# Attention and feed-forward on one core: split probabilities transposed by VectorE blocks and SBUF-to-SBUF transfers instead of TensorE

## The chip, the cores and the metric

One NeuronCore of one Trainium2 chip runs the whole program; the other cores are idle. The metric is the device time of one execution in microseconds, as the median of three runs. Engines are named as the profile names them: PE (TensorE matmuls), PEld (TensorE weight loads), DVE (VectorE), ACT (ScalarE), POOL (GpSimd) and SP (SyncE, which issues all DMAs here).

## The reference

Eight batches of eight heads, 576 rows of 64, in float32. Each row of scores keeps only entries within `tau` of its maximum; the attention output, with heads side by side, is 4608 tokens of 512 and goes through a feed-forward layer of width 2048:

```python
scores = scale * np.matmul(q, k.transpose(0, 1, 3, 2))
thresh = np.max(scores, axis=-1, keepdims=True) - tau
scores = np.where(scores >= thresh, scores, -1000000000.0)
scores = scores - np.max(scores, axis=-1, keepdims=True)
attn = np.exp(scores)
attn = attn / (np.sum(attn, axis=-1, keepdims=True) + 1e-09)
attn_out = np.matmul(attn, v)                     # then heads are concatenated: x
r = np.maximum(x @ w_in, 0.0)
out = (s * (r * r) + b) @ w_out
```

## The kernel before

**Number format.** Most operands are split into a high half in the format fp32r and a low half (value minus high half, also fp32r), and a product is the sum of two or three fp32r matmuls. Batch 0 alone is computed with plain float32 matmuls ("plain" tiles), while the weights are still being loaded and split; batches 1 to 7 use "split" tiles.

**Tiles.** A tile is 128 query rows of one head against all 576 keys. There are 288 tiles: 36 plain, 252 split. A batch has two halves of 256 query rows per head, and 64 tail rows per head; two heads' tails share one tile. For each tile, in `tile_of`: PE computes the scores (L329); DVE moves them to `sm`, negated and scaled, with the row minimum (L332), and adds `tau` to it (L335); ACT takes the exponential into `em` (L338); DVE masks it and sums the row (L341), and takes the reciprocal and a small clipping term (L344, L346); POOL normalizes `em` (L349); PE transposes `em` in four blocks of 128x128 and one of 128x64 into the PSUM banks `tp` and `tt` (L358, L359). For a split tile ACT copies the transposed block to the high half (L389, L391) and DVE subtracts it to get the low half (L392, L394). `with_v` multiplies a group of 256 or 320 query columns with v: nine matmuls (L405), of which the last takes the last 64 keys with both halves side by side; ACT and DVE add the two halves of the result (L410, L412).

**Heads.** `Head.load` and `Head.prepare` load k (twice, on both halves of the partitions), q and v of a head, and split them: k on ACT and POOL (L279, L280), q on ACT and DVE (L287, L288), v on ACT and POOL (L292, L293). This is done anew for each half of a batch, so 112 times.

**Feed-forward.** A `Block` takes 256 tokens (18 blocks, 288 steps of 128 hidden units). A step is twelve matmuls of 256 columns (L536) into the bank `h`, three ACT operations (L539, L541, L542), the low half on POOL (L543; on DVE in the last block) and six matmuls of 512 columns (L549). `finish` scales the sum on DVE (L560) and stores it.

**Order.** Each engine runs its instructions in a fixed order. `Plan` makes it before the program is built: every operation has an engine, a planned duration, the keys that it reads and writes, and a due time counted in tiles (`at`); the planner runs through simulated time and gives each engine, when it is free, the ready operation that is due first. DMAs are planned on SP the same way. Operations with `port=True` and all POOL operations are planned never to overlap (L92 to L94); `dve2` sets that mark:

```python
    def dve2(cost, fn, r, w, at):
        plan.add("DVE", cost, fn, r, w, at, True)
```

On the chip nothing but semaphores between dependent operations is left of the plan, and the order. `LOAD_AHEAD`, `PREPARE_AHEAD`, `VALUES_AFTER` and `FFN_AFTER` shift the due times of loads, splits, `with_v` and feed-forward blocks; `each` spaces the steps of a block.

Of the kernel before, what the change touches and what calls it, by code (L numbers as in the profile page):

```python
# [9 lines left out]
F32 = mybir.dt.float32  # L10
# [5 lines left out]

LOAD_AHEAD, PREPARE_AHEAD = 6, 2.5  # L20
SCORES_AHEAD, VALUES_AFTER = 1, 1
FFN_AFTER = 1.5


# [3 lines left out]
FIRST_WEIGHTS = 4  # L28

# [78 lines left out]
def tile_attention_ffn(ctx: ExitStack, tc: tile.TileContext, qT, kT, v, tau, w_in, w_out, s, b, out):  # L108


# [14 lines left out]
    HS = S // 2  # L125

# [19 lines left out]
    st = [const(f"st{i}", [P, 8]) for i in range(6)]
    smem = [tuple(const(f"{n}{i}", [P, S + 1]) for n in ("sm", "em")) for i in range(2)]
    qs = [const(f"q{j}", [P, NB], F32R) for j in range(2)]
    raw_head = const("rk", [P, S]), const("rq", [P, S]), const("rv", [P, 5, D])
    xb = [const(f"x{i}", [P, NC, NB]) for i in range(3)]  # L150
    xt = const("xt", [P, NC, 4 * T])
    oo = const("oo", [P, 2, DM])
# [3 lines left out]
        ("s", [P, 2, 512]), ("o", [P, 2, DM]), ("tp", [P, NQ, P]), ("tt", [P, 512]), ("pv", [P, 512]), ("h", [P, 512]))}  # L156
# [4 lines left out]
    def claim(keys, fn):  # L161

        old = [k for k in list(plan.writer) + list(plan.readers) if isinstance(k, tuple) and k[0] == keys[0]]
        plan.add("-", (0, 0), fn, [], list(dict.fromkeys(old)) + keys, -100)


    def split_buffers():
        def e():
            t = sb("e", [P, 9, 3 * P], F32R)
            lazy["ehi"], lazy["elo"] = t[:, 0:5], t[:, 5:9]  # L170

        def k():
            lazy["k"] = sb("k", [P, 4, S], F32R)

        def v_():
            lazy["v"] = sb("v", [P, 3, 5, 2, D], F32R)
        claim(["e"] + [(n, c) for n in ("eh", "el", "et") for c in range(6)], e)
        claim(["k", "khi0", "klo0", "khi1", "klo1"], k)
        claim(["v", "v0", "v1", "v2"], v_)
        claim(["e32", "oo0", "oo1"] + [("x", 2, c, j, u) for c in range(NC) for j in range(2) for u in range(2)], lambda: None)  # L180

    def pe(n, cols, fn, r, w, at):

        plan.add("PE", (n * (0.44 * cols + 6.5), n * (0.44 * cols + 6.5) + 170), fn, r, w, at)
# [4 lines left out]
    def dve2(cost, fn, r, w, at):  # L189
        plan.add("DVE", cost, fn, r, w, at, True)  # L190
# [9 lines left out]


    class Plain:


        def __init__(self, bi, p_):
            self.bi, self.p, self.tag = bi, p_, ("w%d" % (NF - 1), "v", "k", "e")[p_]
            self.keys = [(self.tag, n) for n in ("k", "q", "v0", "v1")]

        def get(self):
            if self not in lazy:  # L210
                t = sb(self.tag, [P, 2 * S - T + 10 * D], F32)
# [18 lines left out]
        def load_tail(self, at):  # L230
            for j in range(2):
                dma(16, lambda j=j: nc.sync.dma_start(
                    out=qd[self.p % 2][j * D:(j + 1) * D, j * T:(j + 1) * T], in_=qT[self.bi, 2 * self.p + j, :, M:S]),
                    [f"qd{self.p % 2}"], [(f"qd{self.p % 2}", j)], at)

    class Head:
        def __init__(self, i, bi, h, q0, q1, tail):
            self.i, self.bi, self.h, self.j, self.q0, self.q1, self.tail = i, bi, h, h % 2, q0, q1, tail

        def load(self, at):  # L240

            q0, q1 = self.q0, self.q1
            rk, rq, rv = raw_head
            self.parts = [], [], []

            def put(which, name, buf, cols, ap, kb):
                for o in 0, D:
                    keys = [(name, o, c) for c in range(cols.start // T, cols.stop // T)]
                    self.parts[which].extend(keys)
                    dma(kb, lambda o=o: nc.sync.dma_start(out=buf[o:o + D, cols], in_=ap), [], keys, at)  # L250
# [7 lines left out]
            dma(128, lambda: nc.sync.dma_start(out=rv[:, 0:NQ, :],
                                               in_=v[self.bi, self.h, 0:M, :].rearrange("(p t) d -> p t d", t=NQ)),
                [], [("rv", 0)], at)  # L260
            for o in 0, D:
                self.parts[2].append(("rv", 1 + o))
                dma(16, lambda o=o: nc.sync.dma_start(out=rv[o:o + D, NQ, :], in_=v[self.bi, self.h, M:S, :]),
                    [], [("rv", 1 + o)], at)

        def prepare(self, at):
            pk, pq, pv_ = self.parts
            j = self.j
            rk, rq, rv = raw_head
            q0, m = self.q0, self.q1  # L270
            self.kks, self.kqs, self.kts = [f"khi{j}", f"klo{j}"], [f"q{j}"], [f"qt{j}"]

            def khi():
                return lazy["k"][:, 2 * j]

            def klo():
                return lazy["k"][:, 2 * j + 1]
            self.q, self.ks = (lambda: qs[j]), (lambda: [khi(), klo()])
            act((580, 675), lambda: nc.scalar.copy(out=khi(), in_=rk), pk, [f"khi{j}"], at)  # L279
# [156 lines left out]

    def weights(f, at):

# [344 lines left out]
```

## Time and profile before

| | |
|---|---|
| median of three runs | 1404.68 us (1398.01, 1405.58, 1404.68) |
| span of the profiled execution | 1402.1 us (the page gives no other time of that execution) |
| PE, PEld busy | 99%, 89% |
| DVE, ACT, POOL busy | 76%, 70%, 53% |
| DMA engines | 23.5% on the kernel's queue, 71 GB/s |

The page shows one execution. A group row gives an engine's instructions of one line: how often, the busy time, the mean duration, then the idle time just before them and what ended it. Durations of PE matmuls overlap, since matmuls are pipelined: what one costs is the distance from its start to the start of the next. A window row gives the busy time of each engine in one stretch of the span, with the number of instructions.

### The profile page before, as it was taken

Reading aid. Unit: us, or ns where it says so; the run is one execution under the profiler, and the core shown is the slowest. Engines: PE = TensorE matmul, PEld = TensorE weight load, DVE = VectorE, ACT = ScalarE, POOL = GpSimd, SP = SyncE. Lnnn points to the kernel's source line nnn. Section 1 sums busy time; section 2 is a strip of 40 time slices with the busy share of each in tenths; the row PEclk is TensorE's granted clock in tenths of the full one; section 3 lists DMA queues with packets and bytes.
Section 4 is the critical chain, followed back from the end, with each engine's and each line's share of the span. In section 5 each row is a group of like instructions: output and inputs, shape, how many; then the busy total and the mean of one; then the engine's idle time right before and its main releaser. Section 6 shows DMA issues by size and latency. Waiting matters only on the chain.

```text
span 1402.1 us, 29393 instructions
## 1 busy us (share of the span) xinstructions
PE 1384.8 (99%) x9369; PEld 1252.3 (89%) x9369; DVE 1066.8 (76%) x3099; ACT 986.8 (70%) x2487; POOL 736.3 (53%) x798
## 2 busy tenths in 40 slices
PE   9999999999999999999999999999999999999998
PEld 7678789889899989998999999999999999999887
DVE  4977568988998898878888787888788887887101
ACT  3777557867777777777777777777777777776443
POOL 1233336656676656655566555665566555564210
PEclk9999999999999999999999999999999999999999
DMA  9701112221222222222122122222222222220000
GB/s 301 248 26 35 29 39 66 82 74 55 79 74 87 63 76 70 81 60 70 52 84 72 55 73 64 83 60 66 65 71 71 70 66 72 64 75 15 16 16 16
DMA packets 94539, 99.59 MB, mean 71 GB/s; under 512 B 34480, under 2 KB 72368, under 8 KB 94384
## 3 DMA queue, kind: packets, MB, share of 16 engines
q1 hardware_dynamic: 94384, 97.71, 23.5%
q8 instruction: 74, 1.21, 0.4%
q14 instruction: 81, 0.66, 0.1%
HBM read 88.21 MB, written 9.44 MB: 70 GB/s over the span
## 4 chain that ended last, share of the span: by engine, by line
PE 93%; DVE 3%; ACT 2%; issue 1%; POOL 0%; DMA 0%; DVEq 0%; SPq 0%; ACTq 0%; POOLq 0%
PE h L536 28%; PE o L549 28%; PE s L329 12%; PE pv L405 9%; PE tp L358 9%; PE pv L374 3%; PE tt L359 2%; DVE em L341 1%; PE h L677 1%; PE h L488 1%; PE o L329 1%; DVE sm L332 1%; DVE e L392 0%; ACT em L338 0%; ACT g L539 0%
## 5 line engine op out<-in xcount | busy, mean ns | idle before, releaser
L536 PE MATMUL h<-xh,w 128*128 128x256 f32 x2304 | 465.5, 285 | 5.0 <-ACT g L539 4.8
L349 POOL TENSOR_SCALAR em<-em,st 128x576 f32<-128x576 f32 x288 | 251.9, 875 | 273.3 <-DVE st L346 113.2
L536 PEld LDWEIGHTS h<-xh,w 128*128 128x128 f32 x2304 | 376.4, 190 | 15.8 <-ACT g L539 8.9
L549 PE MATMUL o<-w,gh 128*128 128x512 f32 x1152 | 369.6, 402 | 0.6 <-ACT g L539 0.5
L543 POOL TENSOR_TENSOR gl<-g,gh 128x256 fp32r<-128x256 f32 x272 | 217.4, 799 | 263.8 <-ACT gh L542 93.6
L536 PE MATMUL h<-xl,w 128*128 128x256 f32 x1152 | 325.4, 282 | 0.2
L341 DVE SCALAR_TENSOR_TENSOR em<-sm,st,em 128x577 f32<-128x577 f32 x288 | 255.3, 887 | 34.5 <-ACT em L338 25.8
L332 DVE TENSOR_SCALAR_CACHE_REDUCE sm<-s 128x576 f32<-128x576 f32 x280 | 211.2, 754 | 89.2 <-PE s L329 86.9
L338 ACT ACTIVATE em<-sm,st 128x576 f32<-128x576 f32 x288 | 224.9, 781 | 49.2 <-DVE sm L332 44.6
L539 ACT ACTIVATE g<-h 128x256 f32<-128x256 f32 x288 | 109.1, 379 | 187.6 <-PE h L536 184.2
L549 PE MATMUL o<-w,gl 128*128 128x512 f32 x576 | 225.9, 392 | 0.1
L536 PEld LDWEIGHTS h<-xl,w 128*128 128x128 f32 x1152 | 219.1, 190 | 5.7 <-DVE xl L521 0.6
L549 PEld LDWEIGHTS o<-w,gh 128*128 128x128 f32 x1152 | 196.4, 189 | 25.9 <-ACT g L539 0.8
L392 DVE TENSOR_TENSOR e<-tp,e 128x512 fp32r<-128x512 f32 (+1 forms) x280 | 178.0, 636 | 53.7 <-ACT e L389 50.0
L389 ACT CAST e<-tp 128x512 fp32r<-128x512 f32 (+1 forms) x280 | 150.5, 538 | 64.3 <-PE tp L358 59.9
L280 POOL TENSOR_TENSOR k<-rk,k 128x576 fp32r<-128x576 f32 x112 | 169.7, 1515 | 45.3 <-ACT k L279 41.9
L358 PE MATMUL tp<-ident,em 128*128 128x128 f32 x1152 | 175.2, 275 | 1.9 <-POOL em L349 0.8
L329 PE MATMUL s<-k,q 128*128 128x288 f32 x896 | 165.4, 306 | 0.3 <-DVE sm L332 0.3
L358 PEld LDWEIGHTS tp<-ident,em 128*128 128x128 f32 x1152 | 137.1, 140 | 26.3 <-issue 5.4
L405 PE MATMUL pv<-e,v 128*128 128x320 f32 (+1 forms) x1008 | 152.6, 296 | 0.0
L405 PEld LDWEIGHTS pv<-e,v 128*128 128x128 f32 x1008 | 141.4, 189 | 2.3
L329 PEld LDWEIGHTS s<-k,q 128*128 128x128 f32 x896 | 130.1, 189 | 4.4 <-DVE sm L332 0.9
(108 smaller groups left out, 1799.3 us busy)
## 6 DMA issues: line engine op xcount, KB each, us to landing
rk<-in_k_dram SPq DMA_DIRECT2D x224, 144.0 KB, 2.8
rv<-in_v_dram SPq DMA_DIRECT2D x112, 128.0 KB, 2.1
rq<-in_q_dram SPq DMA_DIRECT2D x168, 64.0 KB, 2.3
w<-in_moe_w_in_dram SPq DMA_DIRECT2D x16, 512.0 KB, 8.6
w<-in_moe_w_out_dram SPq DMA_DIRECT2D x16, 512.0 KB, 8.7
out_dram<-oo SPq DMA_DIRECT2D x32, 256.0 KB, 2.2
rq<-in_q_dram SPq DMA_DIRECT2D x56, 80.0 KB, 2.4
rv<-in_v_dram SPq DMA_DIRECT2D x224, 16.0 KB, 2.0
```

Source lines behind the costliest of these rows:

```text
L280: pool((1420, 1450), lambda: nc.gpsimd.tensor_tensor(out=klo(), in0=rk, in1=khi().bitcast(F32), op=ALU.subtract), pk + [f"khi{j}"], [f"klo ...
L329: nc.tensor.matmul(ps[:, hf, 0:HS], stat, kk[:, cs], start=(n == 0), stop=(n == len(seq) - 1))
L332: dve((760, 840), lambda: nc.vector.tensor_scalar(out=get()[0][:, 0:S].rearrange("p (a b) -> p a b", a=2), in0=ps[:, :, 0:HS], scalar1=-SC ...
L338: act((690, 785), lambda: nc.scalar.activation(out=get()[1][:, 0:S], in_=get()[0][:, 0:S], func=AF.Exp, bias=st8[:, 0:1], scale=-1.0), [sm ...
L341: dve2((830, 930), lambda: nc.vector.scalar_tensor_tensor(out=get()[1], in0=get()[0], scalar=st8[:, 1:2], in1=get()[1], op0=ALU.is_le, op1 ...
L349: pool((800, 835), lambda: nc.gpsimd.tensor_scalar(out=get()[1][:, 0:S], in0=get()[1][:, 0:S], scalar1=st8[:, 4:5], scalar2=st8[:, 5:6], o ...
L358: nc.tensor.transpose(out=tp[:, t, :], in_=em[:, t * P:(t + 1) * P], identity=ident)
L392: dve((60 + 560 * big, 140 + 560 * big), lambda hi=hi, lo=lo, cs=cs: nc.vector.tensor_tensor(out=lo(), in0=tp[:, :, cs], in1=hi()[:, 0:NQ] ...
L405: nc.tensor.matmul(ps, g.hd.v()[:, kt, :, :], o[:, kt], start=(n == 0), stop=(n == len(seq) - 1))
L536: nc.tensor.matmul(ps, w[:, c, :], x[:, c, :], start=(i == 0), stop=(i == 3 * NC - 1))
L543: do((715, 750), lambda: eng.tensor_tensor(out=lo, in0=g, in1=hi.bitcast(F32), op=ALU.subtract), [f"g{k}", f"gh{k}"], [f"gl{k}"], at)
L549: nc.tensor.matmul(bank["o"][:, t, :], a[:, ts_], w, start=(f == 0 and i == 0), stop=(f == NF - 1 and i == 2))
```

## The change

For split tiles the PE transposes and their PSUM evacuations go. DVE transposes `em` in 32x32 blocks into `tr`; four DMAs from SBUF to SBUF (32 partitions with four pieces of 640 bytes each, to 128 partitions) put the blocks of 32 queries into place in `er`; ACT copies all 128x640 of it to the high half `eh`, and POOL subtracts in place, so `er` becomes the low half. `with_v` has ten matmuls. `er` and `eh` have five slots of a tile. Plain tiles keep the PE transposes.

The two halves of a batch are now processed together (`ONCE`: half 1, half 0, tail of head 0, then head 1), so k and v of a head are loaded and split once, except in batch 7 (`TWICE`, 64 heads in all). The low half of k moves from POOL to DVE. v is loaded in pieces of 256 bytes rather than 1 KB. One buffer `raw` holds first k, then q of a head. The addition of `tau` moves from DVE to ACT, L346 goes, and the scale is applied in the split of q.

In PSUM, `h` and `tp` take turns for the first product of a step and `pv` and `tt` for `with_v`; the split block input `xh`, `xl` and the output row buffer `oo` have one buffer in place of two. Weights are converted in the memory of `er` and `eh`. The planned durations are other ones, `dve2` no longer marks the port, and the due times of `with_v` and the feed-forward are later.

```diff
-SCORES_AHEAD, VALUES_AFTER = 1, 1
-FFN_AFTER = 1.5
+SCORES_AHEAD, VALUES_AFTER = 1, 2
+FFN_AFTER = 2.5
+TWICE = (7,)
...
     def dve2(cost, fn, r, w, at):
-        plan.add("DVE", cost, fn, r, w, at, True)
+        plan.add("DVE", cost, fn, r, w, at)
...
+            act((673, 760), lambda: nc.scalar.copy(out=lazy["k"][:, 2 * j], in_=raw), self.rk, [khi], at)
+            dve2((760, 830), lambda: nc.vector.tensor_tensor(
+                out=lazy["k"][:, 2 * j + 1], in0=raw, in1=lazy["k"][:, 2 * j].bitcast(F32), op=ALU.subtract),
+                self.rk + [khi], [klo], at)
...
+        act((200, 280), lambda: nc.scalar.activation(out=st8[:, 1:2], in_=st8[:, 0:1], func=AF.Identity, bias=tau0),
+            [(ks_, 0), "nsc"], [(ks_, 1)], i - 0.4)
...
+        def blocks():
+            nc.vector.transpose(out=to[:, :, 0:NQ].rearrange("p m c q -> p m (c q)"),
+                                in_=ev[:, 0:M].rearrange("p (m r) -> p m r", m=4))
+            nc.vector.transpose(out=to[:, 0:2, NQ], in_=ev[:, M:S].rearrange("p (m q) -> p m q", m=2))
+        dve((740, 810), blocks, [em_k], [tr_k], i + 0.5)
+        t = ti.slot
+        for n in range(4):
+            plan.add("SP", (450, 2600), lambda n=n: nc.sync.dma_start(
+                out=lazy["er"][:, 4 * t + n].bitcast(F32),
+                in_=to[32 * n:32 * n + 32].rearrange("p m c q -> p m (c q)")), [tr_k], [("er", t, n)], i + 0.5)
...
+        act((730, 820), lambda: nc.scalar.copy(out=hi(), in_=lo().bitcast(F32)), ker, [("eh", t)], i + 1)
+        pool((1640, 1670), lambda: nc.gpsimd.tensor_tensor(
+            out=lo(), in0=lo().bitcast(F32), in1=hi().bitcast(F32), op=ALU.subtract), [("eh", t)], ker, i + 1)
...
+            seq = [(kt, o) for kt in range(5) for o in (hi, lo)]
...
+    ONCE = [(0, 1), (0, 0), ("T",), (1, 0), (1, 1)]
+    HALF = [[(0, 0), ("T",), (1, 0)], [(0, 1), (1, 1)]]
...
+            each = 1.65 if i < 60 else 0.75 if 140 < i < 150 else 1.1
```

More of the change, by code (lines that the diff above doesn't have):

```diff
@@ L538, in step, with products @@
-            pe(3 * NC, NB, products, kx + [(f"w{f}", "i")], ["h"], at)
-            act((290, 385), lambda: nc.scalar.activation(out=g, in_=ps, func=AF.Relu), ["h"], [f"g{k}"], at)
+            ps, g, hi, lo = bank[hb][:, 0:NB], gb[k], gh[k], gl[k]
+            def products(cs):
+                xh, xl = xhl()
+                for c in cs:
+                    for i, (w, x) in enumerate(((wi[0][f], xh), (wi[0][f], xl), (wi[1][f], xh))):
+                        nc.tensor.matmul(ps, w[:, c, :], x[:, c, :], start=(c == 0 and i == 0), stop=(c == NC - 1 and i == 2))
@@ L627, in half, with plain_tiles @@
+    pairs = [Plain(0, p_) for p_ in range(NP)]
+    def plain_tiles(pair, u):
+        A, tiles, fl = pairs[pair], [], slice(0, P)
+        xk = xbuf(0, u)
+        for j in range(2):
             for i in range(2):
                 ti = Tile_()
-                c = i * P
-                ti.st = lambda hd=hd, c=c: [(hd.q()[:, c:c + P], kk) for kk in hd.ks()]
-                ti.kq = lambda hd=hd: hd.kks + hd.kqs
-                ti.heads, ti.plain, ti.blocks = [hd], None, []
-                ti.parts = [(g, i * P, fl)]
@@ L634, in half @@
-                ti.end = [g] if i == 1 and not (more and hd is A) else []
+                c, r = u * NB + i * P, slice(j * D, (j + 1) * D)
+                ti.st = lambda c=c, r=r: [(A.get()[1][r, c:c + P], A.get()[0][r])]
+                ti.kq = lambda: A.keys[:2]
+                ti.plain = [(A, j, fl, xb[xk][:, pair, i * P:(i + 1) * P], ("x", xk, pair, j, i))]
+                ti.heads, ti.blocks, ti.end = [A], [], []
                 tiles.append(ti)
-            if more and hd is A:
+            if u and not j:
@@ L643, in half @@
+                ti.plain = [(A, h, slice(h * T, (h + 1) * T), xt[:, pair, 0:T], ("xt", 0, pair, h)) for h in range(2)]
+                ti.heads, ti.blocks, ti.end = [A], [], []
                 tiles.append(ti)
-        half(A)
-        half(Bh)
         if pair == NP - 1:
-            blocks = tiles[-1].blocks
-            blocks += [("full", bi, u)]
-            if t1 == 4 and bi % 4 == 3:
-                blocks.insert(0 if bi == B - 1 else len(blocks), ("tail", bi // 4, 0))
-        return tiles
@@ L654, in tile_attention_ffn @@
-    pairs = [Plain(0, p_) for p_ in range(NP)]
-    heads = [Head(2 * vi + j, vis[0], 2 * vis[1] + j, vis[2] * P, vis[3] * P, vis[4])
-             for vi, vis in enumerate(visits) for j in range(2)]
-    tiles, first = [], {}
-    for vi, vis in enumerate(visits):
-        for ti in make_tiles(vis, *((pairs[vis[1]],) * 2 if vis[0] == 0 else heads[2 * vi:2 * vi + 2])):
-            for hd in ti.heads:
-                first.setdefault(hd, len(tiles))
-            tiles.append(ti)
+            tiles[-1].blocks = [("full", 0, u)]
```

513 lines of the change are left out of this document (265 added, 248 removed).

## The prediction

> **What bounds the kernel now.** First the busy time by stages, to see whether one engine holds throughout. The columns are the stretch, its length, then each engine's busy time.
>
> ```profile
> core 0: us, PE busy (x) PEld busy (x) DVE busy (x) ACT busy (x) POOL busy (x), PEclk, DMA share, GB/s
> 0.00:208.00 208.00, 202.15 (x1182) 153.69 (x1183) 141.22 (x398) 131.87 (x303) 63.33 (x79) 1.00 0.35 114
> 208.00:650.00 442.00, 437.34 (x3051) 406.39 (x3050) 383.95 (x1127) 329.94 (x850) 279.72 (x290) 1.00 0.25 72
> 650.00:1250.00 600.00, 599.55 (x4194) 560.17 (x4193) 491.43 (x1437) 449.14 (x1142) 357.76 (x386) 1.00 0.24 69
> 1300.00:1402.00 102.00, 95.84 (x603) 85.66 (x601) 14.20 (x28) 42.39 (x105) 12.65 (x17) 1.00 0.05 16
> ```
>
> From 208 us on, PE is busy with hardly a gap, at the full granted clock: 0.45 us are missing from 600 in the steady stage, 4.7 from 442 in the stage before, where DVE is fuller (87% against 82%). The last 102 us hold little but feed-forward. Since busy PE time is modelled, I checked it with the chain of work that ended last. It lies on PE for 93% of the span:
>
> ```profile
> PE 93%; DVE 3%; ACT 2%; issue 1%; POOL 0%; DMA 0%; DVEq 0%; SPq 0%; ACTq 0%; POOLq 0%
> ```
>
> So PE's work sets the time, and a matmul taken out is worth its distance to the next one, as long as nothing else takes over. To see what could, I read the groups of the steady stage (650 to 1250 us) engine by engine: first DVE, then POOL, then ACT.
>
> ```profile
> L341 DVE SCALAR_TENSOR_TENSOR em<-sm,st,em 128x577 f32<-128x577 f32 x133 | 116.1, 873 | 10.7 <-ACT em L338 5.5 <-DVE st L335 0.5
> L332 DVE TENSOR_SCALAR_CACHE_REDUCE sm<-s 128x576 f32<-128x576 f32 x134 | 101.2, 755 | 37.2 <-PE s L329 35.7
> L392 DVE TENSOR_TENSOR e<-tp,e 128x512 fp32r<-128x512 f32 (+1 forms) x147 | 93.8, 638 | 28.0 <-ACT e L389 25.8
> L394 DVE TENSOR_TENSOR e<-tt,e 64x128 fp32r<-64x128 f32 (+1 forms) x147 | 39.9, 271 | 5.1 <-ACT e L391 0.5
> L288 DVE TENSOR_TENSOR q<-rq,q 64x256 fp32r<-64x256 f32 x59 | 37.4, 634 | 1.8
> L335 DVE TENSOR_SCALAR st<-st,tau_t 128x1 f32<-128x1 f32 x133 | 27.9, 210 | 2.8
> L412 DVE TENSOR_TENSOR x<-pv,x 64x256 f32<-64x256 f32 x59 | 24.9, 421 | 13.0 <-ACT x L410 8.0 <-ACT xt L410 2.4 <-PE tt L359 1.1
> L344 DVE RECIPROCAL st<-st 128x1 f32<-128x1 f32 x133 | 21.3, 160 | 6.2 <-DVE em L341 0.5
> L346 DVE TENSOR_SCALAR st<-st 128x1 f32<-128x1 f32 x133 | 17.7, 133 | 0.0
> ```
>
> ```profile
> L349 POOL TENSOR_SCALAR em<-em,st 128x576 f32<-128x576 f32 x133 | 113.3, 852 | 103.0 <-PE h L536 38.9 <-DVE st L346 19.7 <-PE s L329 12.5
> L543 POOL TENSOR_TENSOR gl<-g,gh 128x256 fp32r<-128x256 f32 x134 | 106.6, 796 | 109.4 <-ACT gh L542 38.6 <-issue 35.2 <-ACT e L391 18.7
> L280 POOL TENSOR_TENSOR k<-rk,k 128x576 fp32r<-128x576 f32 x60 | 88.1, 1469 | 24.8 <-ACT k L279 24.3 <-PE h L536 0.5
> L293 POOL TENSOR_TENSOR v<-rv,v 128x320 fp32r<-128x320 f32 x59 | 54.4, 922 | 6.9 <-ACT v L292 6.1
> ```
>
> ```profile
> L338 ACT ACTIVATE em<-sm,st 128x576 f32<-128x576 f32 x133 | 104.0, 782 | 20.7 <-DVE sm L332 18.3 <-POOL k L280 1.3 <-POOL em L349 0.9
> L389 ACT CAST e<-tp 128x512 fp32r<-128x512 f32 (+1 forms) x147 | 79.3, 540 | 40.0 <-PE tp L358 37.8 <-DVE st L335 0.7 <-DVE em L341 0.6
> ```
>
> ```profile
> L279 ACT CAST k<-rk 128x576 fp32r<-128x576 f32 x60 | 40.4, 673 | 0.1
> L391 ACT CAST e<-tt 64x128 fp32r<-64x128 f32 (+1 forms) x147 | 36.5, 249 | 0.0
> ```
>
> The stage holds 133 tiles (L349) and 134 feed-forward steps (L543), so a tile with its step takes 600/133 = 4.51 us, and of that DVE is busy 491.43/133 = 3.69 us, ACT 3.38, POOL 2.69.
>
> **PE, the sum's first terms.** What a matmul occupies is read from the timeline, start to next start.
>
> ```profile
> 799.77 0.60 PE L358 MATMUL tp<-ident,em 128*128 128x128 f32 x4
> 800.21 0.27 PE L359 MATMUL tt<-ident,em 128*64 128x128 f32 x1
> 800.24 0.78 PE L329 MATMUL s<-k,q 128*128 128x288 f32 x4
> ```
>
> ```profile
> 806.72 1.48 PE L405 MATMUL pv<-e,v 128*128 128x320 f32 x9
> 808.04 0.39 PE L549 MATMUL o<-w,gh 128*128 128x512 f32 x1
> ```
>
> The five transposes of a tile hold PE from 799.77 to 800.24, so 0.47 us; 252 split tiles lose 252 x 0.47 = -118 us. A tenth matmul per group comes in: 1.32/9 = 0.147 us at 320 columns, so about 0.12 at 256, with 56 groups of each: +15 us. Scores and feed-forward keep their matmuls. PE's floor is 1402.1 - 118 + 15 = 1299 us; per tile with one step, 4.51 - 0.47 + 15/252 = 4.10 us.
>
> **The other engines, against 4.10 us per tile.**
>
> DVE loses L392, L394, L335 and L346: 179.3/133 = 1.35 us per tile. It gains two block transposes, of 512 and of 64 columns, an operation that the trace doesn't show. Bounds: the cheapest DVE rows (0.42 at 512 columns, L469 below, and 0.13, L346) make 0.55; the dearest (0.87, L341, and 0.27, L394) make 1.14. I take 0.9, from the ordinary price of 512 columns (0.69, L521 below) and somewhat under L394 for the small one. The low half of k, from L521 by width, is 0.75 us x 64/252 heads per tile = 0.19. DVE comes to 3.69 - 1.35 + 0.9 + 0.19 = 3.43 us, 84% (3.08 to 3.67).
>
> ```profile
> L469 DVE TENSOR_SCALAR xh<-xh 128x512 int32<-128x512 int32 x16 | 6.5, 419 | 0.3 <-ACT xh L466 0.3
> L521 DVE TENSOR_TENSOR xl<-x,xh 128x512 fp32r<-128x512 f32 x16 | 10.9, 686 | 0.2
> ```
>
> POOL gains a subtraction of 640 columns: 796 ns at 256 and 1469 at 576 extend to 1.60 us. (Bounds: 0.95 by L349's rate for one input, 1.84 by L293's.) It loses k (88.1/133 = 0.66) and some of v (54.4/133 = 0.41 becomes 0.922 x 64/252 = 0.23): 2.69 + 1.60 - 0.66 - 0.18 = 3.45 us, 84% (2.80 to 3.69). L349 keeps its size; its second scalar costs nothing that I count.
>
> ACT loses L389, L391 (115.8/133 = 0.87) and 48 of 112 heads' k (0.13; v is less), gains the copy of 640 columns (0.73, L279 by width; 0.54 to 0.87 by L389 and L338) and the addition of tau (0.2, under the smallest row, L391): 3.38 - 1.00 + 0.93 = 3.31 us, 81%.
>
> SP issues four DMAs more per tile and loses part of the loads; I count some 1470 for the split tiles, 5.8 per tile. An issue takes 0.33 to 0.59 us (first fence below), so 1.9 to 3.4 us; I take 3.2, 78%. Each of the four waits for the transposes. Behind it in SP's order stand the next head's loads, for which ACT's and DVE's splits wait; these are due 2.5 tiles ahead, some 10 us, and that hides it. A transfer of 80 KB lands 2.1 to 2.8 us after its issue (second fence); ACT's copy waits for all four, and behind it on ACT stand exponentials and the feed-forward's L539, for which PE waits. Transposes to low half take some 8 us. `VALUES_AFTER` of two tiles and the five slots hide that; without this cover each tile would show part of it (third rival). DMA engines are at 24%, and the smaller pieces of v are no term.
>
> ```profile
> 808.98 0.59 SPq L250 DMA_DIRECT2D rk<-in_k_dram  x1
> 810.08 0.33 SPq L258 DMA_DIRECT2D rv<-in_v_dram  x1
> ```
>
> ```profile
> rk<-in_k_dram SPq DMA_DIRECT2D x224, 144.0 KB, 2.8
> rv<-in_v_dram SPq DMA_DIRECT2D x112, 128.0 KB, 2.1
> ```
>
> The remaining edits: second PSUM banks remove waits of PE, of which the steady stage has hardly any. The single `oo` makes the second block of rows wait for the store of the first, 2.1 + 0.6 us, shown at the end and a little where the last blocks change: +4 us; earlier, scores and other products hide it. The single `xh`, `xl` is hidden by the second products of the last two steps. The front (0 to 208 us) keeps its loads and plain tiles: 0, between -10 and +10.
>
> **What leaks.** DVE and POOL don't run freely beside each other. The next fence pairs a DVE instruction with two SBUF inputs with a POOL instruction, twice; the one after it shows two POOL instructions undisturbed.
>
> ```profile
> 251.81 1.97 DVE L341 SCALAR_TENSOR_TENSOR em<-sm,st,em 128x577 f32<-128x577 f32 x1
> 251.74 1.43 POOL L280 TENSOR_TENSOR k<-rk,k 128x576 fp32r<-128x576 f32 x1 [0.35 <-POOL v L293]
> 226.91 0.82 DVE L341 SCALAR_TENSOR_TENSOR em<-sm,st,em 128x577 f32<-128x577 f32 x1
> 227.12 1.22 POOL L543 TENSOR_TENSOR gl<-g,gh 128x256 fp32r<-128x256 f32 x1 [0.92 <-ACT gh L542]
> ```
>
> ```profile
> 800.04 0.82 POOL L349 TENSOR_SCALAR em<-em,st 128x576 f32<-128x576 f32 x1 [1.76 <-PE h L536]
> 801.79 0.74 POOL L543 TENSOR_TENSOR gl<-g,gh 128x256 fp32r<-128x256 f32 x1 [0.93 <-ACT e L391]
> ```
>
> L341, 0.82 us when it is first, started behind POOL in the first pair and ended 0.61 us after POOL's end (253.78 against 253.17). In the second pair POOL, 0.74 us undisturbed, ended 0.61 after DVE (228.34 against 227.73). So each holds something that the other needs, for all but 0.21 us of a DVE and 0.13 us of a POOL instruction. L288 shows the price: 634 ns, where L412 of the same width, with an input in PSUM, takes 421. Undisturbed durations per new tile: POOL 0.82 + 1.57 + 0.74 + 0.23 = 3.36 us in 3.25 instructions (1.57 is 1.43 extended to 640 columns); DVE 0.82 (L341) + 0.19 (k) + 0.23 (q at 0.42, tails at half) + 0.10 (L521, 36 in 252 tiles) = 1.34 us. Held: 3.36 - 0.42, and 0.61 + 0.14 + 0.10 + 0.07 on DVE, together 3.86 of 4.10 us, 94%. Today's count, made likewise, is 2.99 of 4.51, 66%. The plan, too, no longer keeps the two apart (`dve2`). I add 0.3 us of waiting per tile to each engine (0 to 0.6, no meeting and every meeting at half a hold): DVE 3.73, POOL 3.75, both 91%. Between the two middle stages of the first fence PE lost one point for five points of DVE; nine points more are 1.8%, and as much for POOL: 3.6% of 4.10 us, 0.15 x 252 = +37 us.
>
> The Trainium skill (SBUF — State Buffer, "Who interferes with whom") says that GpSimd and a Vector instruction with two SBUF inputs exclude each other, the later one blocked for the whole instruction. The trace agrees on the exclusion; on its length it shows 0.61 of 0.82 us, and I go by that. In full, the rule would make the second rival.
>
> **Sum:** 1402.1 - 118 + 15 + 37 + 4 = 1340 us. The median of the runs is 2.6 us above the profiled span, so **1343 us** (1308 to 1390).
>
> **Rivals.**
>
> *PE loses nothing* (0.27). The waits fall into slack: 1299 + 4 + 2.6, less some of the 4.7 us lost between 208 and 650 us: 1303 (1290 to 1308). For it: at 82% DVE, PE lost 0.1%. Against: two engines at 84% or more and the shared hold at 94% at once.
>
> *The port decides* (0.10). If POOL's and DVE's instructions exclude each other for their whole length, a tile needs 3.36 + 1.34 = 4.70 us. The mechanism sits between L341, q's and k's subtraction on one side and every POOL instruction on the other; it decides from 4.10 us on, and above 4.51 the change loses: 1402.1 + 0.19 x 252 + 4 + 2.6 = 1457, slower. The page named above gives this result. For it: both pairs. Against: their 0.61 us.
>
> *The way through SP and ACT decides* (0.09). If ACT's order has the copy of a tile ahead of the exponential two tiles on, a loop closes: four issues 2.2, landing 2.1, copy 0.73, L338 0.78, L341 0.87, L344 0.16, L349 0.85, transposes 0.9, waits 0.6: 9.2 us for two tiles, 4.6 each. That is 1299 + 0.50 x 252 + 4 + 2.6 = 1432, slower. With three tiles in the loop it is 3.1 us a tile and costs nothing; nothing in the trace says which.
>
> *The block transposes take twice 0.9 us* (0.06). DVE needs 3.73 + 0.9 = 4.63 us a tile: 1299 + 0.53 x 252 + 6.6 = 1439. No row shows the operation.
>
> **Chances and range.** The forecast has 0.48. A measurement here can't tell 0.5% (7 us) from no change. Faster: 0.48 + 0.27, less 0.03 for the forecast's upper end: 0.72. The last three make 0.25; 0.04 of it is for milder shapes of them that end level, so slower is 0.21 and the same 0.07. The range goes from PE's floor, with its early loss regained, to the loop: 1290 to 1435. Outside are the port in full and the transposes (0.16), and a little below the floor.
>
> **What would show it.** No PE transposes in split tiles, and 1120 matmuls in `with_v`. Right, if in the middle a tile with one step takes 4.2 to 4.3 us, with POOL and DVE near 90%, the mean of L341 near 1.1 us, the two transposes near 0.9 together and an SP issue of 0.33 to 0.6. Wrong, if PE has no gaps (first rival), if POOL or DVE is full while PE waits for low halves or scores (second, fourth), or if ACT waits for the transfers in each tile (third).

## The result, and the profile after

The changed kernel takes 1648.49 us (median of four runs, 1645.36 to 1649.29) against 1401.35 us before: a ratio of 1.1755 with a 95% interval of 1.1717 to 1.1793. It is slower by 247 us, where 1343 us were forecast. The profiled execution's span is 1643.5 us.

The busy time by stages, first, in the same stretches as for the kernel before:

```profile
core 0: us, PE busy (x) PEld busy (x) DVE busy (x) ACT busy (x) POOL busy (x), PEclk, DMA share, GB/s
0.00:208.00 208.00, 194.19 (x1177) 147.74 (x1177) 146.67 (x338) 141.00 (x339) 103.55 (x80) 0.99 0.36 116
208.00:650.00 442.00, 352.84 (x2037) 309.30 (x2036) 349.36 (x796) 281.17 (x647) 394.13 (x271) 0.89 0.43 108
650.00:1250.00 600.00, 490.10 (x2954) 426.17 (x2952) 421.77 (x946) 372.78 (x864) 495.68 (x352) 0.95 0.38 96
```

PE was busy for 599.55 of 600 us; now it is for 490. Its granted clock, 1.00 in every stretch before, is 0.89 and 0.95. POOL is now the fullest engine, 89% and 83%. The chain of work that ended last, which lay on PE for 93%, can be followed back for only 6% of the span here, so it names no engine:

```profile
PE 6%; DMA 0%; DVE 0%; POOL 0%; issue 0%; ACT 0%; SPq 0%; ACTq 0%; DVEq 0%; POOLq 0%
```

The groups of the steady stage (650 to 1250 us) that answer to those of the prediction:

```profile
L340 POOL TENSOR_SCALAR em<-em,st 128x576 f32<-128x576 f32 x108 | 208.5, 1932 | 38.6 <-DVE st L339 28.9 <-ACT g L527 3.4 <-ACT eh L387 2.6
L388 POOL TENSOR_TENSOR er<-er,eh 128x640 fp32r<-128x640 f32 x109 | 179.1, 1645 | 23.3 <-ACT eh L387 21.9 <-PE tp L518 1.0 <-DMA er<-tr 0.2
L529 POOL TENSOR_TENSOR gl<-g,gh 128x256 fp32r<-128x256 f32 x111 | 96.2, 872 | 38.0 <-PE o L535 22.9 <-issue 7.7 <-ACT gh L528 6.5
L336 DVE SCALAR_TENSOR_TENSOR em<-sm,st,em 128x577 f32<-128x577 f32 x108 | 131.3, 1217 | 12.8 <-ACT st L331 8.6 <-ACT em L333 3.7
L371 DVE STREAM_TRANSPOSE tr<-em 128x512 f32<-128x512 f32 x107 | 76.1, 711 | 94.6 <-POOL em L340 88.9 <-DMA er<-tr 5.3
L373 DVE STREAM_TRANSPOSE tr<-em 128x64 f32<-128x64 f32 x107 | 21.7, 202 | 0.0
L387 ACT CAST eh<-er 128x640 fp32r<-128x640 f32 x108 | 78.1, 723 | 55.5 <-DMA er<-tr 54.6
```

A tile with its step takes 600/108 = 5.56 us, where 4.25 were forecast (4.10 and a leak of 0.15). One row stands out: the normalization, 852 ns before at L349, takes 1932 at L340, on the same tile of 128x576. DVE's transposition waits 88.9 us for it in this stage. From the timeline, one such instruction, and four issues of SP:

```profile
1005.02 1.72 POOL L340 TENSOR_SCALAR em<-em,st 128x576 f32<-128x576 f32 x1
1005.37 2.55 SPq L377 DMA_DIRECT2D er<-tr  x4
```

### The profile page after: what moved, and what is told of

Read it like the earlier page. It is cut to its first block, busy times and chain, and to the rows that moved or that the text cites. A ratio compares the mean times of both kernels' runs of the same rounds, so it can differ in the third digit from the quotient of the medians.

```text
span 1643.5 us, 27906 instructions
## 1 busy us (share of the span) xinstructions
PE 1376.1 (84%) x8221; PEld 1183.7 (72%) x8221; DVE 1119.3 (68%) x2533; ACT 1016.8 (62%) x2371; POOL 1240.6 (75%) x893
## 3 DMA queue, kind: packets, MB, share of 16 engines
q8 instruction: 66, 1.08, 0.3%
## 5 line engine op out<-in xcount | busy, mean ns | idle before, releaser
L340 POOL TENSOR_SCALAR em<-em,st 128x576 f32<-128x576 f32 x288 | 557.8, 1938 | 164.4 <-DVE st L339 118.8
L388 POOL TENSOR_TENSOR er<-er,eh 128x640 fp32r<-128x640 f32 x252 | 409.5, 1627 | 55.8 <-ACT eh L387 53.4
L371 DVE STREAM_TRANSPOSE tr<-em 128x512 f32<-128x512 f32 x252 | 179.2, 711 | 217.2 <-POOL em L340 202.8
L518 PE MATMUL h<-xh,w 128*128 128x256 f32 x1280 | 270.8, 292 | 9.8 <-ACT g L525 5.2
L387 ACT CAST eh<-er 128x640 fp32r<-128x640 f32 x252 | 182.3, 724 | 141.4 <-DMA er<-tr 136.5
L518 PEld LDWEIGHTS h<-xh,w 128*128 128x128 f32 x1280 | 219.5, 198 | 16.9 <-ACT g L525 7.5
L518 PE MATMUL tp<-xh,w 128*128 128x256 f32 x1024 | 208.7, 286 | 0.7 <-ACT g L525 0.6
L518 PE MATMUL h<-xl,w 128*128 128x256 f32 x640 | 187.9, 294 | 18.5 <-DVE xl L504 18.4
L518 PEld LDWEIGHTS tp<-xh,w 128*128 128x128 f32 x1024 | 171.3, 194 | 3.2 <-ACT g L525 1.1
L518 PE MATMUL tp<-xl,w 128*128 128x256 f32 x512 | 146.1, 285 | 0.0
```

The costliest lines, as they stand in the source:

```text
L340: pool((870, 900), lambda: nc.gpsimd.tensor_scalar(out=ev, in0=ev, scalar1=st8[:, 4:5], scalar2=None, op0=ALU.mult), [em_k, (ks_, 4)], [em ...
L371: nc.vector.transpose(out=to[:, :, 0:NQ].rearrange("p m c q -> p m (c q)"), in_=ev[:, 0:M].rearrange("p (m r) -> p m r", m=4))
L387: act((730, 820), lambda: nc.scalar.copy(out=hi(), in_=lo().bitcast(F32)), ker, [("eh", t)], i + 1)
L388: pool((1640, 1670), lambda: nc.gpsimd.tensor_tensor(out=lo(), in0=lo().bitcast(F32), in1=hi().bitcast(F32), op=ALU.subtract), [("eh", t)] ...
L518: nc.tensor.matmul(ps, w[:, c, :], x[:, c, :], start=(c == 0 and i == 0), stop=(c == NC - 1 and i == 2))
```

## The experiments

**1. The normalization with one scalar or two.** In the kernel before it multiplied by one scalar per row and added another, in the change it only multiplies. Given the second scalar again (a column of zeros):

```diff
-            out=ev, in0=ev, scalar1=st8[:, 4:5], scalar2=None, op0=ALU.mult), [em_k, (ks_, 4)], [em_k], i)
+            out=ev, in0=ev, scalar1=st8[:, 4:5], scalar2=zero, op0=ALU.mult, op1=ALU.add), [em_k, (ks_, 4)], [em_k], i)
```

> The changed kernel with one thing put back: POOL's normalization multiplies by the reciprocal and adds a second scalar per row, here zero, as in the kernel before (multiply and add in one instruction), so the result is the same. Theory A, the one-scalar form of this POOL instruction is slow by itself (1.72 us undisturbed in the trace after, 0.82 before) and makes POOL the bound: the instruction returns to 0.82 to 0.9 us, POOL loses 288 x 0.9 = 260 us of work, and the time falls to what the prediction said, 1343 us, between 1303 and 1420. Rival B, the instruction is long because it waits for VectorE: it stays above 1.5 us and the time stays above 1600 us. Rival C, the instruction becomes short but the rest of the change binds anyway (the shared port, or the way through SP and ACT): 1430 to 1600 us.

Measured: 1541.85 us, ratio to before 1.1025 (1.0991 to 1.1059). That is 107 us less than the change, and still 199 above the forecast, in the band that stood for a second cause beside the slow form. Its steady part, 400 to 1300 us (180 tiles and 181 steps), and three of its groups there:

```profile
400.00:1300.00 900.00, 787.60 (x4862) 702.35 (x4861) 702.12 (x1594) 614.77 (x1437) 680.71 (x585) 0.95 0.42 107
L341 POOL TENSOR_SCALAR em<-em,st,zero 128x576 f32<-128x576 f32 x180 | 194.0, 1078 | 71.2 <-DVE st L340 59.1 <-ACT gh L529 2.8 <-ACT eh L388 2.6
L337 DVE SCALAR_TENSOR_TENSOR em<-sm,st,em 128x577 f32<-128x577 f32 x181 | 210.9, 1167 | 28.0 <-ACT st L332 16.4 <-ACT em L334 10.4
L388 ACT CAST eh<-er 128x640 fp32r<-128x640 f32 x182 | 132.0, 725 | 119.1 <-DMA er<-tr 116.4 <-issue 1.8
```

POOL's normalization is back near its old size; PE is still idle for 112 of 900 us. What its matmuls waited for there (in all, times, longest; the largest six of thirteen lines):

```profile
PE s L325 <- DVE sm L328: 39.7, 39, 2.9
PE h L519 <- DVE xl L505: 12.3, 7, 3.0
PE o L536 <- POOL gl L530: 9.9, 16, 1.3
PE o L536 <- DVE oo L547: 9.7, 3, 4.2
PE pv L403 <- POOL er L389: 8.5, 10, 1.9
PE tt L403 <- POOL er L389: 7.9, 12, 1.2
```

Over all thirteen lines, results of DVE make up 72 of the 112 us and results of POOL 26.

**2. The same edit alone, in the kernel before.** The multiply-add of L349 becomes a multiply; the clipping term is left out of the result.

```diff
-            out=get()[1][:, 0:S], in0=get()[1][:, 0:S], scalar1=st8[:, 4:5], scalar2=st8[:, 5:6], op0=ALU.mult,
-            op1=ALU.add), [em_k, (ks_, 4), (ks_, 5)], [em_k], i)
+            out=get()[1][:, 0:S], in0=get()[1][:, 0:S], scalar1=st8[:, 4:5], scalar2=None,
+            op0=ALU.mult), [em_k, (ks_, 4), (ks_, 5)], [em_k], i)
```

> The kernel before with only the second scalar of POOL's normalization taken away (the clipping term is left out of the result; VectorE still computes it). Theory A: the instruction goes from 0.82 to 1.72 us undisturbed; POOL's share in the middle rises from 60% to about 80%, and the kernel gets slower by 1 to 6% (1415 to 1490 us), since PE has no slack. Rival B: the instruction stays at 0.82 to 0.9 us and the time at 1402.

Measured: 1437.08 us, ratio 1.028 (1.0242 to 1.0317), 40 us more than the kernel before. The row of the edit, 875 ns in the kernel before over the whole span:

```profile
L349 POOL TENSOR_SCALAR em<-em,st 128x576 f32<-128x576 f32 x288 | 508.9, 1767 | 190.9 <-DVE st L346 90.2 <-PE h L536 24.8 <-DVE st L335 12.8
```

**3. The price by itself.** At the end of the kernel before, POOL runs the operation in five forms on one tile, four times over.

```diff
+        probe(scalar1=st0[:, 4:5], scalar2=st0[:, 5:6], op0=ALU.mult, op1=ALU.add)
+        probe(scalar1=st0[:, 4:5], scalar2=None, op0=ALU.mult)
+        probe(scalar1=st0[:, 4:5], scalar2=0.0, op0=ALU.mult, op1=ALU.add)
+        probe(scalar1=1.0, scalar2=None, op0=ALU.mult)
+        probe(scalar1=1.0, scalar2=0.0, op0=ALU.mult, op1=ALU.add)
```

> The kernel before with 20 extra POOL instructions of 128x576 on a buffer that nothing reads any more, at the end, four of each: multiply and add by two scalars per row; multiply by one scalar per row; multiply by a scalar per row and add the constant zero; multiply by a constant; multiply and add by constants. Theory A: the forms with two operations take 0.82 us and those with one 1.72 us, whatever the kind of scalar. A variant of A: only the form with one scalar per row is slow, and one constant is fast. Rival B: all take 0.82 us.

The whole kernel took 1410.68 us with the probes. One round of them in the timeline, the first row being the form with two scalars per row, and the others in the order of the diff:

```profile
1327.47 0.82 POOL L745 TENSOR_SCALAR em<-em,st 128x576 f32<-128x576 f32 x1
1333.86 1.73 POOL L745 TENSOR_SCALAR em<-em,st 128x576 f32<-128x576 f32 x1
1340.26 0.75 POOL L745 TENSOR_SCALAR em<-em,st 128x576 f32<-128x576 f32 x1
1346.65 1.65 POOL L745 TENSOR_SCALAR em<-em 128x576 f32<-128x576 f32 x1
1353.05 0.67 POOL L745 TENSOR_SCALAR em<-em 128x576 f32<-128x576 f32 x1
```

The form with one operation takes 1.65 to 1.73 us and the form with two 0.67 to 0.82, whether the scalars are constants or a column. So it is the number of operations, not the kind of scalar.

**4. The planner's mark for the port**, given back to `dve2` in the changed kernel.

```diff
-        plan.add("DVE", cost, fn, r, w, at)
+        plan.add("DVE", cost, fn, r, w, at, True)
```

> The changed kernel with the port mark of the plan put back on VectorE's two-input operations, so that the plan keeps them apart from POOL's; POOL's normalization keeps its one scalar. Theory A: POOL stays the bound with its 1.72 us, so the time stays within 2% of 1648 us (1615 to 1690). Rival D, that it is the lost mark that costs the time: VectorE's masking falls from 1139 to about 890 ns and the time below 1500 us.

Measured: 1683.6 us, 35 more than the change. The lost mark isn't the cause.

The rest builds on the kernel of experiment 1, at 1541.85 us, and differences in brackets are against it. The runs of one kernel lie 1 to 13 us apart (30 in experiment 14), so a difference of 4 to 14 us is close to none. In its expectations theory A is the hold that POOL and DVE share, B the way through SP, C, E and F the order and the buffer, D that DVE is full.

**5 and 6. Less hold, or a shorter way.** In 5 POOL's subtraction is cut to a fifth of its columns; in 6 the four transfers of a tile become one of the same bytes, without the rearrangement.

```diff
-            out=lo(), in0=lo().bitcast(F32), in1=hi().bitcast(F32), op=ALU.subtract), [("eh", t)], ker, i + 1)
+            out=lo()[:, :, 0:32], in0=lo().bitcast(F32)[:, :, 0:32], in1=hi().bitcast(F32)[:, :, 0:32],
+            op=ALU.subtract), [("eh", t)], ker, i + 1)
```

> Built on the changed kernel with two scalars per row in GpSimd's normalization (1541.85 us). GpSimd's subtraction that makes the low halves works on 32 of each 160 columns instead of all; the order is kept, and the part left out is that the other low halves are wrong. Theory A (GpSimd and VectorE wait for each other in two-input instructions, and GpSimd's 1.62 us per tile is the largest part of it): some 1.25 us per tile of GpSimd go, VectorE's L338 falls from 1.17 to below 1.0 us, and the time falls by 80 to 180 us, to 1360 to 1460. Theory B (the way of the 1008 transfers through SP and the copy on ScalarE holds each tile up): the time stays above 1500.

```diff
-            plan.add("SP", (450, 2600), lambda n=n: nc.sync.dma_start(
-                out=lazy["er"][:, 4 * t + n].bitcast(F32),
-                in_=to[32 * n:32 * n + 32].rearrange("p m c q -> p m (c q)")), [tr_k], [("er", t, n)], i + 0.5)
+            plan.add("SP", (450, 2600), lambda n=n: None if n else nc.sync.dma_start(
+                out=lazy["er"][:, 4 * t:4 * t + 4].bitcast(F32),
+                in_=to.rearrange("p m c q -> p m (c q)")), [tr_k], [("er", t, n)], i + 0.5)
```

> Built on the same kernel of 1541.85 us. The four transfers of a tile become one of the same bytes which leaves every row on its partition; so the rearrangement is left out and three of four issues on SP (0.64 us each) with it. Theory A (shared hold of GpSimd and VectorE): 1510 to 1550, since no engine's work changes. Theory B (the way through SP): the probabilities arrive 1.9 us earlier, ScalarE's 158 us of waiting for them nearly go, and the time falls to 1400 to 1480.

Measured: 1480.85 us (-61) and 1486.9 us (-55). Each gain is smaller than its own theory wanted, and larger than the other theory allowed, so neither theory holds alone. Each edit also changes more than its theory names: 5 takes 316 us of work from POOL (1005.8 to 689.4 us), and 6 takes work from SP, whose DMA issues sum to 634 us between 400 and 1300 us in experiment 1 and to 287 us in 6. The mean of L337 in the two (the expectation of 5 calls it L338), 400 to 1300 us, the fifth of the columns first:

```profile
L337 DVE SCALAR_TENSOR_TENSOR em<-sm,st,em 128x577 f32<-128x577 f32 x187 | 164.9, 883 | 50.4 <-ACT st L332 30.3 <-ACT em L334 18.7
```

```profile
L337 DVE SCALAR_TENSOR_TENSOR em<-sm,st,em 128x577 f32<-128x577 f32 x191 | 223.9, 1174 | 17.0 <-ACT st L332 8.8 <-ACT em L334 6.4
L388 ACT CAST eh<-er 128x640 fp32r<-128x640 f32 x191 | 137.2, 719 | 5.5 <-DMA er<-tr 5.2
```

They work in different places: the first takes DVE's waiting behind POOL away, the second leaves it (1174) and takes ACT's waiting for the transfers away, 5.2 us where the kernel of experiment 1 has 116.4 in the same stretch.

**7. Planned durations as measured**, nothing else (four of twelve changed lines shown, `...` for what is left out).

```diff
-                parts.append((slice(u * NB, (u + 1) * NB), qs[n], f"q{n}", (400, 480), (500, 560)))
+                parts.append((slice(u * NB, (u + 1) * NB), qs[n], f"q{n}", (501, 580), (881, 940)))
...
-        dve2((970, 1040), lambda: nc.vector.scalar_tensor_tensor(
+        dve2((1245, 1310), lambda: nc.vector.scalar_tensor_tensor(
...
-        pool((870, 900), lambda: nc.gpsimd.tensor_scalar(
+        pool((1078, 1110), lambda: nc.gpsimd.tensor_scalar(
...
-            plan.add("SP", (450, 2600), lambda n=n: nc.sync.dma_start(
+            plan.add("SP", (640, 2850), lambda n=n: nc.sync.dma_start(
```

> Built on the same kernel of 1541.85 us. Nothing but the planned durations is changed, to what that kernel's trace shows (for instance 1.25 instead of 0.97 us for VectorE's masking with its sum, 0.88 instead of 0.50 for the low half of q, 1.14 instead of 0.76 for that of k, 0.64 instead of 0.45 for an issue on SP, 1.08 instead of 0.87 for GpSimd's normalization), so that the order of each engine's work is planned with them. Theory C (the fixed order was planned with durations that are too short, so that engines wait in order for work that is late): the time falls by more than 50 us, to below 1490. Theories A and B: within 30 us of 1541.85, 1512 to 1572.

Measured: 1531.33 us (-10.5). Theory C falls: planning with the right durations is worth little. ACT's waiting for the transfers falls to 45.7 us between 400 and 1300 us, from 116.4, so the time doesn't follow that waiting alone.

**8, 9 and 12. POOL's work given to another engine**: the normalization to ACT (8), the low halves to DVE (9), or half of them (12).

```diff
-        pool((870, 900), lambda: nc.gpsimd.tensor_scalar(
-            out=ev, in0=ev, scalar1=st8[:, 4:5], scalar2=zero, op0=ALU.mult, op1=ALU.add), [em_k, (ks_, 4)], [em_k], i)
+        act((780, 860), lambda: nc.scalar.activation(
+            out=ev, in_=ev, func=AF.Copy, scale=st8[:, 4:5]), [em_k, (ks_, 4)], [em_k], i)
```

> Built on the same kernel of 1541.85 us. The normalization leaves GpSimd for ScalarE (one activation with a scale per row, planned at 0.78 us like the exponential of the same size). GpSimd loses 1.08 us per tile, ScalarE gains some 0.77 and comes to about 4.3 us per tile of its own. Theory A (shared hold): VectorE's two-input instructions wait less, and the time falls to 1420 to 1500, ScalarE being the next to bind. Theory B (the way through SP and ScalarE): ScalarE, which the transfers wait for, is later still, and the time rises to 1550 to 1640.

```diff
-        pool((1640, 1670), lambda: nc.gpsimd.tensor_tensor(
+        dve2((860, 930), lambda: nc.vector.tensor_tensor(
```

> Built on the kernel with two scalars per row (1541.85 us). The low halves of the probabilities (1.62 us per tile on GpSimd) are subtracted by VectorE, planned at 0.86 us. Theory A (the hold that GpSimd and VectorE share sets the pace, GpSimd's share of it being the longest): the summed hold falls by some 0.7 us per tile, VectorE's masking falls from 1.17 to below 1.0 us, and the time falls to 1430 to 1520. Theory D (VectorE is what is full, with its waits counted, and any work more on it costs time): VectorE comes to some 4.4 us per tile, and the time is 1540 to 1640.

```diff
+        pool((860, 890), lambda: nc.gpsimd.tensor_tensor(
+            out=lo()[:, 0:2], in0=lo().bitcast(F32)[:, 0:2], in1=hi().bitcast(F32)[:, 0:2], op=ALU.subtract),
+            [("eh", t)], ker[0:2], i + 1)
+        dve2((480, 550), lambda: nc.vector.tensor_tensor(
+            out=lo()[:, 2:4], in0=lo().bitcast(F32)[:, 2:4], in1=hi().bitcast(F32)[:, 2:4], op=ALU.subtract),
+            [("eh", t)], ker[2:4], i + 1)
```

> Built on the same kernel of 1541.85 us. The low halves of a tile are split between GpSimd (320 columns, planned at 0.86 us) and VectorE (320 columns, planned at 0.48). Theory A: GpSimd's hold falls by 0.8 us per tile and VectorE's grows by 0.4; the time is 1480 to 1530. Theory D (VectorE full): 1540 to 1590. If this is faster than with either engine alone, both limits stand side by side.

Measured: 1576.75 (+35), 1573.63 (+32) and 1559.08 us (+17). Experiment 8 lies in theory B's band, 9 and 12 in D's; theory A falls as the one cause. In 9 the exclusion is nearly gone, and the time rises all the same, with PE's wait for DVE's copy of the scores going from 39.7 to 67.2 us between 400 and 1300 us; its busy times, and L337 from 400 to 1300 us:

```profile
PE 1373.2 (88%) x8221; PEld 1196.7 (76%) x8221; DVE 1175.1 (75%) x2785; ACT 1012.2 (65%) x2371; POOL 601.3 (38%) x642
```

```profile
L337 DVE SCALAR_TENSOR_TENSOR em<-sm,st,em 128x577 f32<-128x577 f32 x177 | 154.4, 875 | 11.2 <-ACT st L332 9.5 <-ACT em L334 0.6
```

**11, 15 and 16. Slack, buffer, order.** Due times of the copy, the low half, the products and the second part one tile later (11); a second pair of banks for the scores (15); both, with the durations of experiment 7 (16).

```diff
-SCORES_AHEAD, VALUES_AFTER = 1, 2
-FFN_AFTER = 2.5
+SCORES_AHEAD, VALUES_AFTER = 1, 3
+FFN_AFTER = 3.5
```

> Built on the same kernel of 1541.85 us. Nothing but due times is changed: the copy of the high halves and the subtraction of the low halves are due one tile later (i + 2), the products with v at 3 instead of 2 tiles after their last tile, the steps of the second part 3.5 instead of 2.5 after. Theory E (the way from the transposition over SP, ScalarE and GpSimd is too long for the slack that the order gives it, so that each engine waits in order): ScalarE's 158 us of waiting for the transfers fall below 60, and the time falls to 1440 to 1510. Theory A (shared hold): 1520 to 1560.

```diff
-        ti.tag = "o" if i < TWO_BANKS and i % 2 else "s"
+        ti.tag = "o" if i < TWO_BANKS and i % 2 else "s2" if i > n_plain + 1 and i % 2 else "s"
```

> Built on the kernel with two scalars per row (1541.85 us), nothing left out. The scores of every other tile go to a second pair of banks; the products with v and the first products of the second part have one bank each instead of two. Theory F (VectorE's lateness reaches TensorE through the single buffer of the scores): TensorE's wait for VectorE's copy, 66 us, nearly goes and the time falls to 1430 to 1500. Theory D (VectorE's own time per tile is the limit, so that a buffer only moves the wait): 1515 to 1560.

> Built on the same kernel, nothing left out: the second pair of banks for the scores, the planned durations as measured, and the due times one tile later. Theory F or a theory that the order is at fault: 1400 to 1470. Theory D: 1490 to 1540, and VectorE is the busiest engine with TensorE below 92%.

Measured: 1528.18 (-14), 1550.13 (+8) and 1546.3 us (+4). Experiments 11 and 15 lie in the bands of theories A and D; 16 lies above D's, and DVE, at 71%, isn't the busiest engine there, as D had it (PE is, at 87%). None of them gains what a fault of the order or of the buffer would give. In 15 the buffer was traded rather than added: PE's wait for DVE's copy falls from 39.7 to 12.8 us between 400 and 1300 us, but its wait for the one bank `h` behind ACT L526 rises from 3.1 to 33.3 us. So this run doesn't rule theory F out.

**13. DVE's own time.** The transposition of 512 columns is left out.

```diff
-            nc.vector.transpose(out=to[:, :, 0:NQ].rearrange("p m c q -> p m (c q)"),
-                                in_=ev[:, 0:M].rearrange("p (m r) -> p m r", m=4))
```

> Built on the kernel with two scalars per row (1541.85 us). VectorE's transposition of the 512 columns (0.71 us per tile) is left out, and with it the rearrangement of these probabilities; the 64-column one, the transfers and all two-input instructions stay. Theory D (VectorE in order, with its waits counted, is the limit): it loses 0.71 of 4.3 us per tile, and the time falls by 80 to 170 us, to 1370 to 1460. Theory A (the hold that it shares with GpSimd is the limit, not its own time): the two-input instructions stay as they were, and the time falls by less than 50 us, to 1490 to 1550.

Measured: 1500.18 us (-42). This lies in theory A's band and not in D's, against experiments 9 and 12: DVE gives up 124 us of busy time and the kernel a third of that. Neither theory holds in all the runs.

**10 and 14. Several at once**: the fifth of the columns, the one transfer and measured durations (10), and without the large transposition too (14). The edits are those above, with the durations that they leave.

> Built on the same kernel of 1541.85 us: the low halves over a fifth of the columns, one transfer of the same bytes instead of four, and an order planned with the durations that these leave. The other low halves and the rearrangement are left out. Singly the three gave -61, -55 and -10 us, which adds up to 1416. If hold and way through SP are the two things that keep the kernel from the 1299 us of TensorE's own work, and each hides part of the other, the time is 1320 to 1400, with TensorE's granted clock above 0.98. If they are one and the same slack counted twice, 1430 to 1480. If a third limit stands (the single buffer of the scores, with VectorE in order), 1400 to 1450 and TensorE still waits most for VectorE's copy of the scores.

> Built on the kernel of the three (low halves over a fifth of the columns, one transfer for four, planned with measured durations; 1386.57 us). The transposition of 512 columns is left out too, as in the run beside it. If VectorE's lateness is what is left, TensorE has no more to wait for: 1290 to 1330, the granted clock above 0.98, TensorE over 96% busy, which is the 1299 us of TensorE's own work. If the single buffer of the scores or the order is what is left, the time stays above 1350.

Measured: 1386.57 us (1380.36 to 1390.35) and 1328.1 us (1316.5 to 1346.35). The busy times of the two kernels' spans, 1384.6 and 1326.3 us, and what PE waited for most in the second, 400 to 1300 us:

```profile
PE 1306.6 (94%) x8221; PEld 1164.0 (84%) x8221; DVE 981.1 (71%) x2533; ACT 999.0 (72%) x2371; POOL 702.2 (51%) x894
```

```profile
PE 1279.3 (96%) x8221; PEld 1140.6 (86%) x8221; DVE 842.8 (64%) x2281; ACT 990.3 (75%) x2371; POOL 687.9 (52%) x894
PE s L325 <- DVE sm L328: 6.4, 7, 1.5
```

No matmul was taken out in either (8221 each, as in the change). Singly, the four cuts gave 61 + 55 + 10.5 + 41.7 = 168 us; together 1541.85 - 1328.1 = 214 us. So they partly cover one another: a cut is worth more when the others are made too. The kernel of the three lies in the band for hold and way as two things that hide part of each other. The last kernel came where the expectation had it if DVE's lateness was what was left; the mean clock in the three was 0.962, lower than expected, and in the four 0.992.

Nothing tried with the whole computation in it came near the kernel before; 1528 us is the best of them.

## Why the prediction was wrong, point by point

**What held.** PE's floor: by the forecast's terms PE's busy time is 1384.8 - 118 + 15 = 1282 us, and in experiment 14, where little holds PE up, the same matmuls are busy for 1279 us of 1326. The two block transposes were priced at 0.9 us and take 711 + 202 = 913 ns, so the fourth rival falls. POOL's subtraction was put at 1.57 us undisturbed; an undisturbed one in the timeline took 1.56. ACT's copy came to 723 ns, for 0.73. L341's mean was to come near 1.1 us and is 1.17 in experiment 1, 1.22 in the change. And the load of the helpers per tile was close: DVE 702.12/180 = 3.90 us and POOL 680.71/180 = 3.78 in experiment 1, where 3.73 and 3.75 were forecast with their waits; ACT 614.77/180 = 3.42, for 3.31; SP's DMA issues 634/180 = 3.5, for 3.2.

**The first step that failed** is one sentence: "L349 keeps its size; its second scalar costs nothing that I count." It treated taking the second scalar away as a change without a price. The price is +0.9 us for each tile (1.72 or 1.73 us for 0.82), 288 times. With it the forecast's own count for POOL is 3.45 + 0.90 = 4.35 us per tile, more than PE's 4.10. It is 107 us of the 305 by which the forecast missed, shown by undoing it in the change; made alone in the kernel before, where POOL is 53% busy, it costs 40 us. The trace before the change showed only the form with two operations, so this belonged among the costs to be bounded from both sides.

**The second is the leak**, put at +37 us; in experiment 1 it is 1541.85 - (1343 - 37) = 236 us. Its size came from fullness: "PE lost one point for five points of DVE". It is this rule that failed, not the load put into it. At 4.10 us per tile the measured 3.90 and 3.78 us would make DVE 95% and POOL 92% full, 13 and 10 points above 82%, and the rule would give 4.6%, some 48 us. Measured, a tile takes 900/180 = 5.00 us in the steady part of experiment 1, 22% over 4.10; DVE is then only 78% and POOL 76% busy, and yet PE is idle for 12.5%, 0.62 us per tile. The rest of the 0.90 us over 4.10 is PE's own busy time, 787.60/180 = 4.38 us per tile at a clock of 0.95; the forecast had no term for the clock. The two stages that the rule was drawn from had a short way from score to product, over PE's transposes. The new way goes through DVE, four issues of SP, ACT and POOL in turn, each with its order fixed, and a delay in one is handed on to the others. This last sentence is argued from the order and the waits; experiments 5, 6 and 13 show that each part of the way costs time, and 14 that they cost most of it together, but no run isolates the handing on.

**The third is the sentence that `VALUES_AFTER` and the five slots hide the way.** They don't: one issue in place of four, with the work of PE, DVE, ACT and POOL left as it was, is worth 55 us. Little of it shows where PE waits for low halves: those waits are 19 of its 112 idle us in experiment 1. The issue was also dearer than taken, 2.55/4 = 0.64 us in the row shown, above the 0.33 to 0.59 of the loads' rows. Not separated: how much of the 55 us is the earlier arrival and how much SP's freed time; and the number of slots was not varied.

**The rivals.** *PE loses nothing* is wrong. *The port decides*: the exclusion is there (L337 falls from 1167 to 883 ns when POOL's longest instruction is cut, to 875 when it leaves POOL), and this agrees with the Trainium skill (SBUF — State Buffer, "Who interferes with whom") on which instructions exclude each other. But experiment 9 takes nearly all of the exclusion away and is 32 us slower, with 66 us more work on DVE. It is a part and not the bound. *The way through SP and ACT* as a loop of two tiles: counted in the trace of experiment 1, of 181 copies 9 have one later exponential ahead of them, 108 have two and 64 three. So the loop mostly closes over three tiles or more. With that kernel's durations it is 2.55 + 2.2 + 0.73 + 0.77 + 1.17 + 0.15 + 1.08 + 0.91 and 0.6 for the handovers, 10.2 us, or 3.4 per tile over three: by this estimate it doesn't set the 5.00. *The single buffers* were no rival, but put at +4 us (`oo`) and at nothing (`xh`, `xl`). In experiment 1 PE waits 9.7 us for the first and 12.3 + 5.0 us for the others between 400 and 1300 us; in experiment 14, where they are still single, 3 us in all. No run gave them back.

**What remains.** Shown: neither the exclusion nor the way is the limit by itself; the four cuts together, which take work from DVE, POOL and SP and shorten the way, give 214 of the 236 us. DVE's share can be estimated from four runs that shift its busy time from 1109.0 us, by +66, +52, -124 and -126 (experiments 9, 12, 13, 5): the time moved by +32, +17, -42 and -61, a third to a half of it. Only 13 leaves POOL's work as it was: experiment 5 takes 316 us from POOL, experiment 9 takes 404 and experiment 12 takes 143. Experiment 8 doesn't fit: DVE's time falls by 52 us, but ACT's rises by 169, and the time by 35. Not settled: how the 214 us divide among them, since the gains overlap; and whether an order of the whole work exists that hides more. Three orders were tried, and none gained more than 14 us.

## What to carry to other kernels

A change that frees the bound engine by sending work through four others isn't costed by how full these are: at 68 to 78% each (DVE 78, POOL 76, SP's issues 70, ACT 68), with fixed orders, they left the bound engine idle for an eighth of the time. Price the way as well, step by step, and ask which single delay along it is not covered; and give a price to every operand that an edit drops, since a simpler form can be the slower one.

## What the runs showed of the hardware that was not expected

POOL's tensor-scalar operation on 128x576 floats takes 1.65 to 1.73 us with one operation and 0.67 to 0.82 with two (experiment 3); adding 0.0 as a second operation made it faster.

PE's granted clock fell in stretches where PE was often idle. A stretch of experiment 1, and what PE waited for most (that row is for 290 to 355 us):

```profile
310.00:335.00 25.00, 12.92 (x47) 10.95 (x48) 20.38 (x50) 13.55 (x28) 16.45 (x13) 0.50 0.41 102
PE s L325 <- DVE sm L328: 12.9, 8, 3.3
```

Over 25 us the clock is 0.50, though PE is busy for half of the time and no wait is longer than 3.3 us; before, it was 1.00 throughout. So idle time was paid for again. The same 8221 matmuls are busy for 1279 us in experiment 14 (mean clock 0.992) and 1352 in experiment 1 (0.949): of the 215 us between these two spans, 143 are idle time and 72 longer busy time. Most of the 72 are slower matmuls: by the trace's record of the clock, PE is busy for 116 us at 0.50 in experiment 1 and for 18 in 14, and if half of that is time lost, the difference is 49 us (an estimate). The Trainium skill (TensorE: Matmul & The Clock Gate, "Part 1: The HAM clock gate") has the clock halved after an idle window of about 3.4 us and full again after a busy one. The 0.50 agrees. In this trace gaps shorter than such a window were enough: the clock first falls here at 289.5 us, and in the 60 us before that no gap between matmuls is longer than 2.0 us.
